# Loading the first queries through ScalarE's queue, without products of ones in gaps, in a newly searched front order

## The chip, the cores and the metric

The kernel runs on one core of a Trainium2 chip. The metric is the device time of one execution in microseconds. A core has TensorE (matrix products; PE in the profile, PEld its weight loads), VectorE (DVE), ScalarE (ACT), GpSimd (POOL) and SyncE (SP, which only issues transfers here). Each engine works through its own list of instructions in order and waits on semaphores of the others. Transfers between the device's memory and the on-chip memory are carried out by 16 DMA engines.

## The reference, cut to what matters

Three layers in a row, in float32, for 2 batches of 768 positions.

```python
# 1: attention, 8 heads of 64: a window of |i-j| < 16, and one summary key and value for each 32 positions
k_sum = k.reshape(B, H, 24, 32, D).max(3);  v_sum = v.reshape(B, H, 24, 32, D).mean(3)
a = softmax([where(window, q @ k.T / 8, -1e9), q @ k_sum.T / 8 + log(32)])
x = a @ [v, v_sum]
# 2: gated layer
u, v = split(relu(x @ w_in));  v = (v - mean(v)) / sqrt(var(v) + 1e-6)
x = (u * (w_spatial @ v + b_spatial)) @ w_out
# 3: gated layer with a 3-tap convolution over positions
h = relu(x @ w_in2);  out = (h * sigmoid(conv3(h))) @ w_out2
```

The weights of layers 2 and 3 come as 64-bit floats; the kernel takes their bits apart itself and holds each as a high and a low float32r part. A product in full precision is three products of such parts.

## The kernel before, in words

**Work of the front.** Attention goes by pairs of heads: pair n (0 to 7; 0 to 3 are batch 0) needs its keys, its queries and its windows of values. `load_kq(n)` loads keys and queries, in two halves each for batch 0 (208 and 192 KB of keys, 192 KB each of queries); `load_values(n)` loads the values' windows in two halves of 288 KB and, for some pairs, the values themselves (384 KB). `keys(n)` scales the windows of keys (L422, L424), takes the maxima of 32 keys (L432) and puts them beside each window (L438). `means(n)` makes the mean values: for pairs 0 and 2 with products on TensorE (L452, for each half of the windows), then L464 and two "puts" (L469, L471), one for each half.

Each pair has two groups; `group(i)` treats six blocks of 64 queries, in these steps:
- scores(i): TensorE, the logarithm and the mask (L496, L503) and q times k (L509), into one of two banks, i mod 2
- row maximum (DVE, L513), six exponentials (ACT, L517), sum and reciprocal (DVE, L520, L523), normalise (L526)
- transposes T(i,0) and T(i,1), three blocks each (PE, L530), into one bank `pt`, each followed by a copy out of it (L552)
- values(i): products with the values (PE, L536), then the high and the low part of the result (L557, L558)

scores(i) needs its bank free, that is the exponentials of group i-2 done; T(i,1) needs the copy of T(i,0) done.

`convert` takes apart one piece of w_in (256 KB for the first four pairs' pieces; L306 load, L307 to L314, L298, L292). Its results feed the products of layer 2 (L344 to L346), which begin while attention still runs and fill TensorE's time between the groups' steps.

**Order.** Every step is entered with `add(engines, rank, reads, writes)` and gets a number. `Plan.order()` emits the steps in the order written in the string `ORDER` (two signs are one number). Each engine's instructions stand in that order. Where a step can run on several engines, `PICK` says on which. The engines' semaphores are set from what is read and written, so that the order decides only who stands behind whom. All loads are steps of "Q", SP's queue.

**Products of ones.** Step 0, `warm(7)`, issues seven products of a tile of ones, 128x512 each, before anything else on TensorE (L1085). Moreover `order()` adds such products in front of a TensorE step where its own cost numbers see TensorE idle for at least 0.5 us, up to the first step of rank 1000 (`plan.fill`):

```python
gap = t - free.get(e, 0.0)
if self.fill and gap >= 0.5:
    n = int((gap - 0.1) / 0.22)
    out.append((free.get(e, 0.0), k, e, 0.22 * n, lambda n=n, f=self.fill[1]: f(n)))
```

In the trace 22 products of ones run: 13 at the start, 5 after scores(0) and 4 after T(1,1).

Of the kernel before, what the change touches and what calls it, by code (L numbers as in the profile page):

```python
# [55 lines left out]
    "AAACABADAFAgAEAiAGAjAZAaAkAhAbAHAqAcAdAeArALBYAfAMBZBbBaBcAIA3A4AsAJAlAtASAUATAVAWAuAvANBiBjAKBEA5A6A7BFCTCRCUBkAmAnAwAx"  # L56
    "AOBvAyAzA8B8CVDJCSBGBwB9DKCbAoApBlBmBnAXDLA9A0A+CcA-BADHDIBxBHBoBRCoBSA1A2BBCdByBzB0BpBqCpBCAYCeAPBdCfCgBDB+DRBrB1B2C1Be"
    "BfBgBhDSEgCqCrCsB3DwEhB-AQCDDeDfB4CEBsChBICWCtBtBuCiDTBKBLEeBJBMBTBNBOCFDgCXCYCjARB5BUCZB6BVCGCHCICJB7C2CAEnETDUDVEoDrCk"
    "CuClCmCnEfCKC3CvCwCaDhDMBPDWBQFNE0DiCxEpCyCzDXC0DYEqErDsCBDxDNDODPBWDjFMDZDaDAC5DtDQFOFPDkDlC6DbDcE1E2DmDnCCDyEUFVDdDoEs"
    "EtDpEuC7C8C9C+C-BXEiDqDBCLFiEvFjE3E4EjEkDzD0EwFvCMCNDuDvCOCPD6DCDDDED7D8D9D1D+D2EEEFD3FBCQEGE5EmDFDGFkEHEIE6D4F6F7EOEPEQ"  # L60
    "ERGmD5F8F9C4FCD-EAEBECFWEXE7FFFGEYEZEaEbGnFHFIFJFKElFXEDE8GlEcEdE9FYFLGkFZFlFaGQGRGDE+ExEJEKELESHPGSGEGFEyFmE-FAFnEzFbFz"
    "F0EMFwGtG6GdEVJwFQFRFcFdF1ENHHHIGeF2F3GfGGGgF4FeHQFSFTF5FoHJFUHRGhGiGjFpFqFrGuFDG7HSHTHKHLEWFsG8GTGUGHF+GVGIFtHMHNFuFfFg"
    "HiHjFxHkHlGJFyG9G+HOHUHXHYGvGKGwHZHVFhHmHWIhGLGMF-GxGyGAHyGBHnIDHzHaGWGXImGCH0FEGoH1HbHcGYHoHqGNGZGaGbHrHsGOGcGPHdG-JtGz"
    "JuIrItIuHtIcG0H2HeGpG1HuIdIiHfIwH3GqG2IsM-INGrJxIOJzGsHvJ3HAIPHBIIHgH4HCInHDG3NBHwG4HEG5IjIvHFIXJ6IJHhJ0IEIYIKNAJ4HGNCIQ"
    "JvIeH5IZJ1IaIbIRIkIFJ5IfIxJyIyIzJBHxJCISJDHpIgILH8I0H+KbJ2H6KBJ8IlITNNKCJEH9H-IMI5H7NDKFI6IBI1I7KDIUIAIoI8JRKcJFKGI9J7NG"
    "NJJGICKHIVKXJ9JHNII2I+I3JSIWJTJUKAKYI-JJJVJIJZJaI4J-JbNEJAJcIpJKKIJWJhKEJLJdJMNFKJNHIqLDJiJeNKLHJXNUJNKQJfIGJjJ+KKJOIHKd"
    "KhJYKRJPJgLIJQKiJmKLLJJoKjNQKSJkKeNLJnLEJpJlJrLFKfKzKlKsKmKtJsKuK0KnKgKZKaLLKMLMK9KTNPLKNMK5LGKkK7LPNOLNK-K+LTNbNRKNLQNS"
    "K6NTNWLXLRLBKvLUNXLOK8LYLZLbKONVNYLVLSNiLcLdNZLALfLgLWNdLeLaKoNeLhLiNaLlLzNcKPNfLCLoL2NpLjKpNgLmNhLpNkL3NlNjLnLkL0L4MOMB"
    "NmJqKqMPMcNnKUMHL1NrNoMQNsNwKrLrNqMINtK1MEMJMRL5MCNuKVMVMdMFNzNvLqNyPXMWKWN3PLMXMDNxK3L6KwL7N0MYN1MeMmPYMnN5K4MfPMMsN2N6"
    "MGK2N4N7LvN+PZPNPaKxN8MoKyN9OAOBMKL9MzMtLsLwN-OCPbMjMuOFPOODPdOHM0PROILxPPMLMkPSOEM7OGOJMpLtPvMqPTMlMrOMPeL+OKPfPQMvOOOL"  # L70
    "OPONOTM3L-MwMxP1P2PpM4OQOUPjMMPkPUPcOaOROWMyLyOVOSMSPlOhPqM5MgM8PVPgP3PWM1MAPmMhOcM9PrOdObM6P7LuP4MZM2MiP8PnQFOXOeM+MaP5"
    "PhPsOkMbQAQGQBPwMNOjL8QCOfOiPiMTMUOoQHQDTXQIP9OYOqOrOpTYOlPtOsQJP+OgPxTdQEP-OmOvPoOtO2PyTeOuPuQXOyP6QYOxQKQcQLQdQMOwOzQZ"
    "O4QaO9O5QeO3PzQbQSQTOnQUQfO6QNQOO-OZQgQVRFO0RAPEQWQPQhPAO7PGO+QuPFP0QQQzO8O1RKQiQjQ0Q1QpTZQvPBQqQRPHQrQsQ2PIQkQwTaQxTjTf"
    "RBRLQlQtRGRcQ3TgQyRCQmQ4TpTrRDRMRHRXRIRNRYQ5TlRZU-RhRiQ6TsQnPCRdThRER2QoTbRJRsRxTiTqRORtRPTcUwRaTkTmT2UxRQQ7RjRyReQ8TtRR"
    "RfTuRzRkR3T3UrPJRTQ9RuPKR4RSR0TnRbQ+RgRlRvR5U1RmSGSLSMT6ToQ-SBRUSfSCR1RwR6PDTvTwR7SDU2SERnSHRVRoRqRpSFU6R8SIR9R+R-UySNSJ"
    "SaSKSbSgRWSORrU7ScVASATCShSQTPTRSdSPTQU8SRSTSkSSTHUzSUSiSVUsSzSlS9SWVBU3U0SmSeS4TSUtSnTJSXVKSYSjSpVLTKSZTxS5TIVDSqSoSrVC"
    "TDS0UuSsS+U9VES1S2TLVMStSuSvVVSxS6S7TTUXVOVGTMTUSwU4URULUdTNS3UlUMVPSyVHU5UYTEUeUSVNUfS-UvT4S8TOUNVWUZVFVgVRUTVXWAVYVrUj"
    "U+TVVcTFVhUUVSV7UVUOVdTAWBT7VIUPV8V3VzV4VQUpVJTGVtViVZVTTWVjVnV0VbWwV1UnWxV5VUTyTzVeVvV6VoV2VmV9VfWCVkT9WDWyW-WEXAV+T-Ua"
    "T5V-UEW1VaWrWMWNW2WFXBUGVlUAWGUmWHUHWzW0WOUkWPWsT0WIVpUgXKVqVsUqWQUhXLWZUoWJT1XDTBWaW6W3WKWTWtXMUbW4XCWuWbXEW7WvXGXHXVXO"
# [1153 lines left out]
```

## Time and profile before

| | |
|---|---|
| three runs | 321.55 us median, 320.36 to 322.11 |
| the profiled execution | 320.81 us; span of its instructions 318.9 us |
| TensorE busy | 311.4 us, 98% of the span |
| VectorE, ScalarE, GpSimd busy | 268.5, 237.3, 117.0 us |
| moved by DMA | 37.64 MB |

The span is the time from the first to the last instruction; 1.9 us of the execution lie around it. A busy share is a mean over the whole span. Each row of the trace starts with its time from the span's start in us and its length in us.

### The profile page before, as it was taken

How to read it: one execution, taken by the hardware profiler on the slowest of the kernel's cores; microseconds unless marked ns; L12 is line 12 of the kernel's file. 1: busy time of each engine (PE TensorE's matmuls, PEld its weight loads, DVE VectorE, ACT ScalarE, POOL GpSimd, SP SyncE). 2: the span in 40 equal slices, each digit the busy share in tenths (PEclk: the TensorE clock that was granted, in tenths of full speed). 3: DMA queues.
4: the chain of work that ended last, by engine and by line, in shares of the span. 5: the costliest groups of instructions: out<-in, count | busy, mean ns of one | idle time of the engine just before them, and what ended most of it. 6: DMA issues, size and time to landing. Idle time of an engine off the chain costs nothing.

```text
span 318.9 us, 6374 instructions
## 1 busy us (share of the span) xinstructions
PE 311.4 (98%) x2376; PEld 271.6 (85%) x2376; DVE 268.5 (84%) x493; ACT 237.3 (74%) x565; POOL 117.0 (37%) x130
## 2 busy tenths in 40 slices
...
GB/s 222 305 266 306 224 218 179 329 93 159 168 189 110 24 2 13 53 29 142 138 114 124 117 134 133 132 2 0 25 21 5 75 25 51 26 99 104 128 140 99
DMA packets 16061, 37.64 MB, mean 118 GB/s; under 512 B 1952, under 2 KB 8480, under 8 KB 16032
## 3 DMA queue, kind: packets, MB, share of 16 engines
...
## 4 chain that ended last, share of the span: by engine, by line
PE 88%; DVE 5%; DMA 2%; SPq 1%; ACT 1%; POOL 1%; issue 1%; DVEq 0%; POOLq 0%
PE late L345 11%; PE late L346 11%; PE late L344 11%; PE mm L344 10%; PE mm L346 9%; PE mm L345 9%; PE pt L530 3%; PE xp L344 3%; PE xp L346 3%; PE xp L345 3%; PE xp L536 3%; PE pt L344 3%; PE pt L346 3%; PE pt L345 3%; PE s L509 2%; DMA a<-q_in 2%
## 5 line engine op out<-in xcount | busy, mean ns | idle before, releaser
L517 ACT ACTIVATE a<-s,a 128x120 f32<-128x120 f32 x96 | 33.3, 379 | 1.0 <-DVE a L513 0.8
L345 PE MATMUL late<-xl,a 128*128 128x512 f32 (+1 forms) x80 | 29.5, 369 | 0.1
L344 PE MATMUL late<-xh,a 128*128 128x512 f32 (+1 forms) x80 | 29.4, 367 | 0.0
L346 PE MATMUL late<-xh,a 128*128 128x512 f32 (+1 forms) x80 | 29.4, 367 | 0.0
L914 DVE SCALAR_TENSOR_TENSOR w<-v,conv_t,w 128x1534 f32<-128x1534 f32 x12 | 21.8, 1817 | 4.4 <-POOL w L908 2.1
...
L526 POOL TENSOR_TENSOR a<-a,a 128x720 f32<-128x720 f32 x14 | 19.4, 1394 | 6.4 <-DVE a L523 3.5
L517 ACT ACTIVATION_READ_ACCUMULATOR a<-s,a 128x1 f32 x96 | 21.6, 225 | 0.0
L292 POOL TENSOR_TENSOR w<-a,w 128x256 fp32r<-128x256 f32 (+2 forms) x13 | 14.2, 1099 | 15.1 <-PE late L345 7.9
L530 PE MATMUL pt<-ident,a 128*120 128x128 f32 x96 | 16.5, 281 | 0.8 <-DVE a L552 0.6
L345 PEld LDWEIGHTS late<-xl,a 128*128 128x128 f32 x80 | 15.0, 188 | 2.4 <-DVE xl L292 0.4
L346 PEld LDWEIGHTS late<-xh,a 128*128 128x128 f32 x80 | 15.0, 188 | 1.9
L344 PEld LDWEIGHTS late<-xh,a 128*128 128x128 f32 x80 | 15.0, 188 | 1.8
L513 DVE TENSOR_REDUCE a<-s 128x6 f32<-128x720 f32 x16 | 14.2, 899 | 2.2 <-PE s L509 2.1
L298 ACT CAST w<-a 128x512 fp32r<-128x512 f32 (+2 forms) x17 | 10.0, 589 | 7.9 <-DVE a L337 3.4
L327 ACT ACTIVATE a<-a 128x512 uint16<-128x512 uint8 x20 | 15.8, 789 | 0.0
L330 ACT ACTIVATE a<-a 128x512 f16<-128x512 f32 x20 | 15.6, 782 | 0.0
L298 ACT CAST xh<-tmp 128x384 fp32r<-128x384 f32 x24 | 12.1, 512 | 3.9 <-DVE tmp L878 2.0
L530 PEld LDWEIGHTS pt<-ident,a 128*120 128x120 f32 x96 | 10.8, 137 | 5.0 <-DVE a L552 1.0
L344 PE MATMUL mm<-w,xh 128*128 128x512 f32 x36 | 14.9, 414 | 0.0
L344 PE MATMUL mm<-xh,a 128*128 128x512 f32 (+1 forms) x40 | 14.7, 367 | 0.0
L346 PE MATMUL mm<-xh,a 128*128 128x512 f32 (+1 forms) x40 | 14.7, 367 | 0.0
...
## 6 DMA issues: line engine op xcount, KB each, us to landing
...
a<-vhalf SPq DMA_DIRECT2D x8, 288.0 KB, 6.9
...
```

What stands on the lines that cost most here:

```text
L292: eng.tensor_tensor(out=lo.r(), in0=src.f(), in1=hi.f(), op=ALU.subtract)
L298: us = {"ACT": (0.2 + n / 1200, lambda: ACT.copy(hi.r(), src.f())), "POOL": (0.12 + n / 1050, lambda: POOL.tensor_copy(hi.r(), src.f()))}
L327: ACT.activation(out=c.ap.bitcast(U16).rearrange("p (n w) -> p n w", w=2)[:, :, 0], in_=byte, func=AF.Copy, scale=1.0 / 32.0, bias=-15.5 / ...
L330: ACT.mul(c.ap.bitcast(F16).rearrange("p (n w) -> p n w", w=2)[:, :, 1], word(), 2.0 ** -60)
L344: PE.matmul(ps, lhsT=lh, rhs=rh, start=first and i == 0, stop=False, **kinds)
L345: PE.matmul(ps, lhsT=lh, rhs=rl, start=False, stop=False, **kinds)
L346: PE.matmul(ps, lhsT=ll, rhs=rh, start=False, stop=last and i == n - 1, **kinds)
L513: DVE.tensor_reduce(out=st[:, 0], in_=sv, op=ALU.max, axis=AX.X, negate=True)
L517: ACT.activation(out=e[:, u, :NK], in_=sv[:, u // GA, u % GA], func=AF.Exp, bias=st[:, 0, u:u + 1], accum_out=sm[:, u, :1])
L526: eng.tensor_tensor(out=e, in0=e, in1=st[:, 1].unsqueeze(2).to_broadcast([128, GB, NK]), op=ALU.mult)
L530: PE.transpose(pt3[:NK, a], e[:, GA * h + a, :NK], ident)
L914: DVE.scalar_tensor_tensor(out=two(ct)[:, bs, to], in0=two(h)[:, bs, of], scalar=scale(k), in1=two(ct)[:, bs, to], op0=ALU.mult, op1=ALU.add)
```

## The change

1. The queries of pair 0 are no longer loaded by SP. Two steps "QA" issue them from ScalarE's instruction list, the first as ScalarE's first instruction.
2. The first use of the exponential, which brings the load of ScalarE's table, becomes a step `table` behind the first of these; the copy of the mask's ones (`one_tile`) waits for it.
3. `plan.fill` goes: no products of ones in gaps. `warm(7)` at the start stays.
4. New strings `ORDER` and `PICK`. With the new step's number counted in, the steps of each engine up to the middle of layer 2's spatial product stand in another order; the last 277 of TensorE's 511 steps stand as before. 78 steps change between VectorE, ScalarE and GpSimd; VectorE gets 461 steps instead of 449, ScalarE 378 instead of 385, GpSimd 116 instead of 120.

SP's loads, before and after, with k for keys, q for queries, v for windows of values, the pair in brackets and the halves as a and b:

```
before: k(0)a k(0)b w_in q(0)a k(1)a k(1)b q(0)b v(0)a w_in q(1)a v(0)b k(2)a k(2)b q(1)b k(3)a q(2)a ...
after:  k(0)a k(0)b k(1)a k(1)b v(0)a w_in w_in q(1)a v(0)b k(2)a k(2)b q(1)b k(3)a q(2)a ...   ScalarE: q(0)a, table, q(0)b
```

TensorE's steps, before and after (means(0)a is the half of the means' products that needs v(0)a):

```
before: warm scores0 scores1 means(0)a scores2 means(0)b T(0,0) scores3 T(0,1) scores4 T(1,0) values0 T(1,1) T(2,0)
        scores5 values1 T(2,1) scores6 T(3,0) mean(1) T(3,1) layer2 scores7 values2 ...
after:  warm scores0 scores1 means(0)a scores2 means(0)b T(0,0) scores3 T(0,1) scores4 T(1,0) values0 T(1,1) scores5
        T(2,0) values1 T(2,1) scores6 T(3,0) mean(1) means(2)a T(3,1) scores7 values2 ...
```

```diff
     def __init__(self):
         self.work, self.seen, self.life = [], {}, {}
-        self.fill = None
...
             if e == "PE":
-                if self.fill and rank >= self.fill[0]:
-                    self.fill = None
-                gap = t - free.get(e, 0.0)
-                if self.fill and gap >= 0.5:
-                    n = int((gap - 0.1) / 0.22)
-                    out.append((free.get(e, 0.0), k, e, 0.22 * n, lambda n=n, f=self.fill[1]: f(n)))
...
         for i in range(qp):
             q0, q1 = S // qp * i, S // qp * (i + 1)
-            dma((q1 - q0) / 2 * 0.84 + (166 if n + i == 0 else 0), lambda q0=q0, q1=q1: SP.dma_start(qts[j].ap[:, q0:q1], q_in[b, p][:, q0:q1]), r - 9 + 1.5 * i, writes=[qts[j].tok(q0, q1)])
+            if n:
+                dma((q1 - q0) / 2 * 0.84, lambda q0=q0, q1=q1: SP.dma_start(qts[j].ap[:, q0:q1], q_in[b, p][:, q0:q1]), r - 9 + 1.5 * i, writes=[qts[j].tok(q0, q1)])
+            else:
+                add({"QA": (1.2 - 0.4 * i, lambda q0=q0, q1=q1: ACT.dma_start(qts[j].ap[:, q0:q1], q_in[b, p][:, q0:q1]))}, r - 100 + i, writes=[qts[j].tok(q0, q1)])
...
     DVE.memset(mhalf, -0.5)
-    ACT.activation(out=stat[0][:, 11:12], in_=mhalf, func=AF.Exp)
...
+    def table():
+        ACT.activation(out=stat[0][:, 11:12], in_=mhalf, func=AF.Exp)
+
...
-    add({"ACT": (2.65, one_tile)}, -99, [tok("ident")], [mask_b.tok(sub="o")])
+    add({"ACT": (2.2, table)}, -99.5, writes=[tok("table")])
+    add({"ACT": (0.6, one_tile)}, -99, [tok("ident"), tok("table")], [mask_b.tok(sub="o")])
...
-    plan.fill = DENSE, warm
```

## Rows read from the trace of the kernel before

**Rows 1.** Part 1 of the page: busy us, share of the span and instructions

```profile
PE 311.4 (98%) x2376; PEld 271.6 (85%) x2376; DVE 268.5 (84%) x493; ACT 237.3 (74%) x565; POOL 117.0 (37%) x130
```

**Rows 2.** Busy us (and instructions) of each engine by stretch, then PEclk, DMA share, GB/s

```profile
2.00:13.05 11.05, 9.61 (x125) 5.11 (x123) 7.40 (x23) 5.99 (x30) 3.96 (x9) 1.00 1.00 279
13.05:17.00 3.95, 3.90 (x78) 3.14 (x82) 3.91 (x9) 3.85 (x18) 3.41 (x5) 1.00 1.02 365
...
40.00:60.00 20.00, 19.89 (x293) 17.29 (x294) 18.50 (x38) 17.82 (x63) 10.10 (x16) 1.00 0.73 232
```

**Rows 3.** The chain that ended last, in order of time: start, us, what

```profile
4.94 7.02 DMA a<-q_in
...
18.68 1.40 POOL a L526
```

**Rows 4.** TensorE in order of time, 0 to 20 us

```profile
1.04 4.55 PE L1085 MATMUL mm<-ones 128*128 128x512 bf16 x13 [1.04 <-DVE mhalf L1079]
...
7.22 1.25 PE L1085 MATMUL mm<-ones 128*128 128x512 bf16 x5
...
13.10 1.49 PE L452 MATMUL mm<-a,a 96*24 96x128 f32 x12 [0.16 <-DMA a<-vhalf]
14.52 0.54 PE L530 MATMUL pt<-ident,a 128*120 128x128 f32 x3
...
18.97 1.03 PE L1085 MATMUL mm<-ones 128*128 128x512 bf16 x4
```

**Rows 5.** TensorE in order of time, 20 to 28 us

```profile
20.60 0.23 PE L496 MATMUL s<-a,ones 64*64 64x72 bf16 x4
...
21.49 0.92 PE L536 MATMUL xp<-a,a 120*64 120x64 f32 x24
...
24.97 0.54 PE L530 MATMUL pt<-ident,a 128*120 128x128 f32 x3 [0.61 <-DVE a L552]
...
26.70 0.92 PE L536 MATMUL xp<-a,a 120*64 120x64 f32 x24
```

**Rows 6.** Transfers issued at 2.10, 4.94 and 5.77 us: KB, us to landing

```profile
a<-q_in SPq DMA_DIRECT2D x1, 192.0 KB, 4.2
...
a<-q_in SPq DMA_DIRECT2D x1, 192.0 KB, 7.0
...
a<-vhalf SPq DMA_DIRECT2D x1, 288.0 KB, 7.3
```

**Rows 7.** SP's issues in order of time: the first two and the eleventh

```profile
0.73 0.86 SPq L397 DMA_DIRECT2D a<-k_in  x2
...
5.77 0.33 SPq L410 DMA_DIRECT2D a<-vhalf  x1
```

**Rows 8.** VectorE and GpSimd in order of time, 14 to 19 us

```profile
14.12 0.97 DVE L432 TENSOR_REDUCE a<-a 128x12 f32<-128x384 f32 x2
15.10 0.56 DVE L552 COPY a<-pt 120x384 f32<-120x384 f32 x1
...
16.04 0.91 DVE L513 TENSOR_REDUCE a<-s 128x6 f32<-128x720 f32 x1
...
16.85 1.74 POOL L471 TENSOR_SCALAR a<-a 24x768 f32<-24x768 f32 x2
```

**Rows 9.** ScalarE in order of time: first and last of the 12 instructions of exponentials(3)

```profile
17.15 0.36 ACT L517 ACTIVATE a<-s,a 128x120 f32<-128x120 f32 x1
...
19.09 0.24 ACT L517 ACTIVATION_READ_ACCUMULATOR a<-s,a 128x1 f32 x1
```

**Rows 10.** Products of ones (L1085) alone, by stretch: us, PE busy, PEld busy, PEclk

```profile
1.04:4.30 3.26, 3.26 (x8) 1.19 (x9) 1.00 0.71 218
7.25:8.40 1.15, 1.15 (x5) 0.37 (x5) 1.00 1.05 258
```

**Rows 11.** TensorE at the end, by stretch: us, PE busy, PEclk

```profile
314.50:318.30 3.80, 0.30 (x2) 1.00 0.33 124
318.45:318.90 0.45, 0.00 (x0) 0.50 0.00 0
```

More of the change, by code (lines that the diff above doesn't have):

```diff
@@ L55 @@
 ORDER = (
[L56 to L79, printed above, removed]
@@ L80 @@
-    "WUWcW8W5WVXNXPXgWWXvXWXXXzXRX3YAWRX4WfT+XFVuX7XSX0T8X5WlUBXYW9YBXhWSXcUcXZUCW+VxXQXiXrWmXdXjX1VwX8WgXnUDX2XIYCX6XoVyUFX9"
-    "WhYDXkYEXtXJX+WnX-XlYMXaYNWXYFUIWLYGUQWdUJXbUKYOXuYHXxXsYIXTWoYPYJXeYTYKXUYQXwYRWiXyWpXmXpWjYZYfYlXfYmUiYgUWWYYLYnYSYoYh"
-    "WeYaYbXqYiYUWkYcYdYpWqYqYVYWYjYXYkYeYY"
+    "ABAIADAJAAAGAHAMACANAKAFAhAEBZAaATAOAjAkALAlArBbAiA4AsBcBaAcAbA5BFBGBdAtAdAPAmA6B9AVAUAuCSBHB+AvAeBjAWAnBIBkBSCVAQAwB-Ax"
+    "CUBwA7AoCTBlA8AyBxCWA9BmApAzA0CcA+ByDKA1BnDLA-BTBABoBBCdA2CeAqDIBzCpC2BpDMA3BCB0BqBDCAARB1CqCEBeCfDJBrEgBsDSCrBEB2BfCgBJ"
@@ new lines @@
+    "CXB3BgBLEhBKChAXCsB4BiBhDfASEfBtC3DTAYCYCtBMCBBNAZBuB5CuBvEiDUDgBOEUDVCZCiCjBPBUCGCaB6CkEoClCFB7B8DhCHCvCmDsEpCwCICbDiCL"
+    "DWCxBQE1DXCnCoCyEqDjCJCzC0C4CCBRDYDNDBFPDtDZFNC1DaDODkDxCKErDyDbC6DlDPEsFQC8CDDQDmDzFODRDcDnDoE2DdEtDuE3EuC7DeBVDpAfC9C+"
+    "EvBWEVC-DqFWFjDADrE4EwEjFwBXFCD0GlD1E5ExAgDvFkEkC5CMDwD7E6FDD8FlGnCNBYCODCCPD9CQDDD+D2FXDEE7D3D4D-CRDFD5F9EYElEFE8D6F8E9"
+    "FYEGEZDGEHEADHFGEBEaGoEbF+FHFZEnEcF0EIECFIF7EdEDE+FmGRFJEeF1EmGEGSE-EyEEEJFAFaEPFKFbF2EQGFFxFnEzFLGmFBERGTF3ESGeE0GUEWEK"
@@ new lines @@
+    "ELFoEMETGGFcFRENFdFMGVF4G7GuFSGfFeEOGgHQFfHRF5FTGhGiF6JxFpHIGHFqHJG8GjFEFrFVF-HKHSGkGIEXG9FyHLFsFUHTFtHMFgHUGvG+HYFzGWFh"
+    "FuFvFiGwGJGKGLHjGAHkGMHZHNInGNGXIoHVGYGBIdHWGDGxIeGZHOHXFFGaG-GyHaJuHlHmGbGCGcIsGzHnHPGOIuGpHbGdHcGPIvG0GQIpG1HzG2GqIxHA"
+    "G3IfHdH0HeHBHCHrGrH1HoItHfH2H3GsHDHsIJIKGtILNAH4HEHtNCHuHgHFHGG4IiHHITJ4HvHwIwHpHqNBIUJ1IVNDHhH5IMJyIqIWIgHxJ2IhIjH6KCG5"
+    "HyIkG6IlNOKDKEH7ImHiKGKHIYINH-H9KcKIIOIZKFH+JzIaIXIbIcKYIPIEIyNEJ7J0KZIQNHJ3H8IzIFNJI0IRIAI6IBISKdI1I2JCJ6I7JSJTJ5JUJ9I3"
@@ new lines @@
+    "IGICI8I9JDJENFJFI4J8NKI+J+IDNGJKJGJaI-JVI5JbJHJWJLNIJMNLJcJAJIJJJBJiJdIrJeJXJNJjKKKJJOKLLEKRKSJfKeJYKTJkJPJZJgIHLFJhJQNM"
+    "JRK0JlKfKMLIJnIIK1JpJmKaKiNRNQJoKmKtKbNNKgJqLJLGNPJsNSJtKjKkKnKoNTLKKlLHKhKuLQLRK6K+K7K-KvLMK8LNK9LOLSLPLTLLKANUNVLUNWNX"
+    "NcNYLVLcNjLALYLdKBNZLWJ-LeKNJvNaLBKULgKOLhLZLXLaKPNeLCLfLbKpNfLiLjNbLmL0KwNdKQNgLDLpL3NqLkKqNhLnNiLqNlL4NmNkLoLlL1L5MPMC"
+    "NnJrKrMQMdNoKVMIL2NsNpMRNtNxKsLsNrMJNuK2MFMKMSL6MDNvKWMWMeMGN0NwLrNzPYMXKXN4PMMYMENyK4L7KxL8N1MZN2MfMnPZMoN6K5MgPNMtN3N7"
@@ new lines @@
+    "MHK3N5N8LwN-PaPOPbKyN9MpKzN+OBOCMLL+M0MuLtLxOAODPcMkMvOGPPOEPeOIM1PSOJLyPQMMMlPTOFM8OHOKMqLuPwMrPUMmMsONPfL-OLPgPRMwOPOM"
+    "OQOOOUM4MAMxMyP2P3PqM5OROVPkMNPlPVPdObOSOXMzLzOWOTMTPmOiPrM6MhM9PWPhP4PXM2MBPnMiOdM+PsOeOcM7P8LvP5MaM3MjP9PoQGOYOfM-MbP6"
+    "PiPtOlMcQBQHQCPxMOOkL9QDOgOjPjMUMVOpQIQETYQJP+OZJwOrOsOqTZOmPuOtQKP-OhPyTeQFQAOnOwPpOuO3PzTfOvPvQYOzP7QZOyQLQdQMQeQNOxO0"
+    "QaO5QbO+O6QfO4P0QcQTQUOoQVQgO7QOQPPAOaQhQWRGO1RBPFQXQQQiPBO8PHO-QvPGP1QRQ0O9O2RLQjQkQ1Q2QqTaQwPCQrQSPIQsQtQ3PJQlQxTbQyTk"
@@ new lines @@
+    "TgRCRMQmQuRHRdQ4ThQzRDQnQ5TqTsRERNRIRYRJRORZQ6TmRaVARiRjQ7TtQoPDReTiRFR3QpTcRKRtRyTjTrRPRuRQTdUxRbTlTnT3UyRRQ8RkRzRfQ9Tu"
+    "RSRgTvR0RlR4T4UsPKRUQ+RvPLR5RTR1ToRcQ-RhRmRwR6U2RnSHSMSNT7TpRASCRVSgSDR2RxR7PETwTxR8SEU3SFRoSIRWRpRrRqSGU7R9SJR+R-SAUzSO"
+    "SKSbSLScShRXSPRsU8SdVBSBTDSiSRTQTSSeSQTRU9SSSUSlSTTIU0SVSjSWUtS0SmS+SXVCU4U1SnSfS5TTUuSoTKSYVLSZSkSqVMTLSaTyS6TJVESrSpSs"
+    "VDTES1UvStS-U+VFS2S3TMVNSuSvSwVWSyS7S8TUUYVPVHTNTVSxU5USUMUeTOS4UmUNVQSzVIU6UZTFUfUTVOUgTAUwT5S9TPUOVXUaVGVhVSUUVYWBVZVs"
@@ new lines @@
+    "UkU-TWVdTGViUVVTV8UWUPVeTBWCT8VJUQV9V4V0V5VRUqVKTHVuVjVaVUTXVkVoV1VcWxV2UoWyV6VVTzT0VfVwV7VpV3VnV+VgWDVlT+WEWzXAWFXBV-UA"
+    "UbT6WAUFW2VbWsWNWOW3WGXCUHVmUBWHUnWIUIW0W1WPUlWQWtT1WJVqUhXLVrVtUrWRUiXMWaUpWKT2XETCWbW7W4WLWUWuXNUcW5XDWvWcXFW8WwXHXIXW"
+    "XPWVWdW9W6WWXOXQXhWXXwXXXYX0XSX4YBWSX5WgT-XGVvX8XTX1T9X6WmUCXZW+YCXiWTXdUdXaUDW-VyXRXjXsWnXeXkX2VxX9WhXoUEX3XJYDX7XpVzUG"
+    "X+WiYEXlYFXuXKX-WoYAXmYNXbYOWYYGUJWMYHURWeUKXcULYPXvYIXyXtYJXUWpYQYKXfYUYLXVYRXxYSWjXzWqXnXqWkYaYgYmXgYnUjYhUXWZYMYoYTYp"
```

5 lines of the change are left out of this document (3 added, 2 removed).

## The prediction

> **What bounds the kernel now.** I read the busy shares first: TensorE works 98% of the span [rows 1], so a gain must come from the little time in which it has nothing to do, or does work that nobody needs. The stretches place that time: between 2.00 and 13.05 us TensorE counts 9.61 us as busy, part of it products of ones, and between 40 and 60 us it is busy 19.89 us of 20, which leaves 0.11 us to take [rows 2]. From there on nothing but its own products orders its time, and their number does not change. So only the front counts, and I read the chain of waits there: SP issues transfers, the tenth of them, q(1)a, takes 7.02 us from 4.94 to 11.96, then scores(2), VectorE, GpSimd's normalise(2) from 18.68 to 20.08 [rows 3], and right behind it T(2,0) on TensorE. The chain does not run over q(0)a, the transfer that the change moves; scores(0) waits for it, but what follows is overtaken by the later landings.
>
> **What TensorE could lose in the front.** Of the products of ones, 5 run at 7.22 for 1.25 us and 4 at 18.97, until normalise(2) lets T(2,0) start at 20.1 [rows 3, 4]; a later stall of 0.61 us stands before T(3,1) at 24.97 [rows 5]. Behind 14.52 that makes about 1.15 + 0.61 = 1.8 us that a better order can take without earlier data. What lies before 14.52 can be taken only if data come earlier: means(0)b starts at 13.10, held by the landing of v(0)b, 5.77 + 7.3 = 13.07 [rows 4, 6, 7], and T(0,0) follows at 14.52.
>
> **The change part by part.**
>
> *q(0) by ScalarE's queue.* Before, q(0)a lands at 2.10 + 4.2 = 6.3 [rows 6]. By ScalarE it can be issued at about 0.73, as SP's first transfer is [rows 7], and share with k(0). The two k(0) halves are 400 KB, with q(0)a 592. At the rate of 279 GB/s [rows 2] the 196,608 bytes of q(0)a delay k(0)b by 0.7 us at most, q(0)b by as much again if it is issued at once. scores(0) then starts some 0.5 us earlier than before. But what bounds the rest is the sum: in both orders exactly the same eleven transfers, 400 + 384 + 400 + 512 + 192 + 576 = 2464 KB, must land before means(0)b can end, and 2176 KB before scores(2). The DMA engines' share between 2.00 and 13.05 is 1.00 [rows 2], so they never rest. If bytes are what counts, q(1)a lands at 11.96 and v(0)b at 13.07 again, and the gain of this part is 0. If instead ScalarE's queue finds room beside SP's, SP has 393,216 bytes less to carry, and both land 393,216 / 279,000 = 1.41 us earlier. A point for room: the rate is 365 GB/s from 13.05 to 17.00 at the same share [rows 2], so a share of 1 is not the highest rate. Bounds: 0 to 1.41 us. I take 0.3, near the lower end, because the share is the row nearest to the case. The Trainium skill ("DMA: Bandwidth & Descriptors", section "Issuing engines are not separate DMA queues") speaks against this edit: transfers issued by several engines run on the same 16 DMA engines and interleave, and only the issuing time is saved. By that rule the landing term is 0 and the sum below 0.3 instead of 0.6.
>
> *ScalarE's own time.* Two issues of 0.43 us each, as SP's pair takes 0.86 [rows 7], go ahead of its copy of the mask's ones and the first windows of keys. These need k(0)b, which lands after 4 us, so it costs nothing; without that cover up to 0.86 us would stand before scores(1).
>
> *w_in behind the first values.* VectorE has a w_in step ahead of the row maximum of group 1. w_in's first piece is now the eighth transfer by bytes and not the third; VectorE, in order, waits with it, and the row maxima and sums behind it wait too. I find row maximum(1) at about 10.2 to 11.1, as late as before, so the earlier scores(0) and scores(1) win nothing there. Price: nothing, as long as scores(2) waits for q(1)a; if that came 1.41 us earlier this would be late next.
>
> *No products of ones.* 6 of the first 13 go; the engine then waits for k(0) and q(0) anyway: 0. The 5 at 7.22 stand before transfers that land later: 0. The 4 at 18.97 fill a wait and are not its cause: 0. What they may keep up, the clock, is a rival below.
>
> *The order behind 13 us, step by step.* VectorE: row maximum(2) ends at 13.9 as before; two maxima of keys 0.97 [rows 8], sum, mean values and reciprocal(1), which I take at 0.6 together, copy 0.56, row maximum(3) 0.91 [rows 8]: ends at 17.0 (before 16.95). ScalarE: exponentials(3) then run from about 17.15 to 19.33 [rows 9], as before. GpSimd: one put (half of 1.74 [rows 8]) moves behind normalise(2), which can end at 17.8 + 1.40 = 19.2 instead of 20.08 [rows 3]. TensorE: scores(5) is now ahead of T(2,0) and fills the hole: it needs its bank, free at 19.33, takes 21.49 - 20.60 = 0.9 [rows 5] and ends at 20.2; T(2,0) ends at 20.7. Before, both were done at 21.49: 0.8 us ahead. Then VectorE, which has the copy of T(2,0) behind row maximum(4) and the parts of values(0), gives some back: T(2,1) about 21.7, scores(6), which needs exponentials(4), about 22.4, T(3,0) 23.3. The mean of pair 1 needs the bank that VectorE reads last for values(1): about 24.3, half a microsecond of stall again. With one half of means(2), 1.4, T(3,1) 0.5 and scores(7) 0.9, values(2) starts at 27.4. Before it starts at 26.70 [rows 5], with 0.54 of layer 2 more and the 1.4 of means(2) less done: at equal work 26.70 - 0.54 + 1.42 = 27.6. The order gains 0.2 to 0.5; I take 0.3. Ends: all 1.8 us of stalls gone, or, if VectorE's 12 steps more (18.50 us of 20 busy from 40 to 60 [rows 2]) open new ones, about -0.8, the part of its idle time there that half a microsecond per ten would use up.
>
> *Tail.* Same order for the last 277 steps; it starts earlier by the front's gain and nothing else.
>
> **Sum.** 0.3 + 0.3 = 0.6 us, against the profiled execution's 320.81: 320.2. The median of the three runs is 0.74 higher, 321.55, so 320.9 for a median. Half a percent, 1.6 us, is about what a measurement here can tell from no change.
>
> **The rivals.**
>
> *A, the forecast:* the same bytes hold the same landings; gain -0.3 to 1.4 us. For it: share 1.00 and the chain through a transfer that waits in the queue [rows 2, 3]. Chance 0.56.
>
> *B, ScalarE's queue finds room:* q(1)a and v(0)b come 1.41 us earlier and TensorE's closed stretch starts at 13.1 instead of 14.5. With the order's 0.3 that is 1.7, with all stalls gone 1.4 + 1.8 = 3.2: 319.8 down to 318.4 for a median. For it: 365 GB/s at the same share [rows 2]; against it: the share itself. Chance 0.26.
>
> *C, slower: TensorE's clock comes up late.* The first eight products of ones take 3.26 us, 0.41 each, and the five from 7.25 on 0.23 [rows 10]: the first run at the 1.2 GHz level, the later at 2.4, though the clock column reads 1.00 in both; it does not record the low level of the start. At the end the granted clock is 0.50, the 1.2 GHz level, at 318.45, with no product after 314.8 [rows 11]. The change leaves seven products, 7 x 0.41 = 2.9 us from 1.04 to 3.9, then a wait to almost 6, and holes of about two microseconds before v(0)a. If the low level still holds when q(1)a lands at 11.96, scores(2) 0.9 and means(0)b 1.42 take twice as long and T(0,0) is 2.3 us late; if it ends between them, 1.1. Minus 0.6 that gives 322.1 to 323.3. It decides from the point where scores(2) itself runs at the low level. The Trainium skill ("TensorE: Matmul & The Clock Gate", "Part 1: The HAM clock gate") says that the slow clock is the default, that activity lifts it and idleness brings it back; the trace shows both ends of that. Against C: scores(0), scores(1) and means(0)a still come in between and pauses of two microseconds are shorter than those 3.6 at the end. Chance 0.10.
>
> *D, the order costs cover:* landings as in A, but VectorE's added steps stall TensorE between 20 and 100 us: -0.2 to -2, some 322.0. Chance 0.08.
>
> **Chances and range.** Faster by over 0.5%: an eighth of A, 0.07, and nearly all of B, 0.23: 0.30. Slower: six tenths of C and half of D, 0.10. The same: 0.60. The range leaves out the far ends of B and C: 318.7 to 322.4.
>
> **What would show it.** Right: q(1)a lands within 0.4 us of 11.96 and v(0)b of 13.07, T(0,0) starts between 14.0 and 14.6, scores(5) before T(2,0) near 19.3, values(2) near 27. Row maximum(1) waits for w_in. B: T(0,0) near 13.1 and the DMA rate between 2 and 12 us above 320 GB/s. C: means(0)b longer than its 1.49 [rows 4]. D: idle times of TensorE behind 28 us, released by VectorE. Wrong also if the landings of k(0)b go beyond 5.5 us, which would put scores(0) later than before.

## The result, and the profile after

The changed kernel takes 323.57 us (median of 8 runs, 322.51 to 324.87) beside 320.74 us of the kernel before (8 runs, 320.00 to 322.11). The ratio is 1.0085, 95% interval 1.0061 to 1.0109: slower by 0.85%, 2.8 us. The prediction, 320.9 us with a range from 318.7 to 322.4 and a chance of 0.1 for slower, is wrong. The profiled execution took 323.84 us, its span is 322.0 us.

The page's first part of the kernel after, busy us and share of the span, answers to [rows 1]:

```profile
PE 311.4 (97%) x2361; PEld 270.4 (84%) x2361; DVE 281.7 (87%) x505; ACT 231.9 (72%) x557; POOL 120.1 (37%) x126
```

TensorE counts 311.4 us as before, although 15 products of ones are gone. VectorE has 12 instructions more and is busy 13.2 us longer. Twelve instructions of half a microsecond would be 6: so others have become longer.

The stretches of the kernel after, in the columns of [rows 2]:

```profile
2.00:13.05 11.05, 9.59 (x127) 6.59 (x126) 8.28 (x22) 6.37 (x30) 5.11 (x10) 1.00 1.04 348
13.05:17.00 3.95, 2.67 (x71) 1.94 (x70) 3.89 (x12) 3.07 (x17) 2.33 (x4) 1.00 0.93 328
40.00:60.00 20.00, 19.50 (x301) 16.60 (x301) 19.29 (x40) 17.85 (x61) 8.49 (x13) 1.00 0.67 218
```

Between 2 and 13.05 us the transfers move 348 GB/s, where it was 279 [rows 2]. TensorE now loses time in the two later stretches: 1.3 us of 3.95, and 0.5 of 20, where VectorE is busy 19.29 us of 20.

The issues of q(0) and q(1)a, and us from issue to landing of the latter and of v(0)b (to set beside [rows 6, 7]):

```profile
0.72 0.41 ACTq L396 DMA_DIRECT2D a<-q_in  x1
...
1.22 0.39 ACTq L396 DMA_DIRECT2D a<-q_in  x1
...
4.34 0.44 SPq L394 DMA_DIRECT2D a<-q_in  x1
```

```profile
a<-q_in SPq DMA_DIRECT2D x1, 192.0 KB, 5.5
...
a<-vhalf SPq DMA_DIRECT2D x1, 288.0 KB, 5.6
```

q(1)a lands at 4.34 + 5.5 = 9.8 (11.96 before), v(0)b, issued at 5.10, at 10.7 (13.07 before). So the landings are 2.1 and 2.4 us earlier, more than rival B's 1.41.

TensorE in order of time, 0 to 16 us, answers to [rows 4]:

```profile
1.04 3.17 PE L1080 MATMUL mm<-ones 128*128 128x512 bf16 x7 [1.04 <-DVE mhalf L1075]
...
5.89 1.48 PE L505 MATMUL s<-a,a 64*64 64x120 f32 x24 [1.23 <-DVE a L434]
...
11.49 1.49 PE L448 MATMUL mm<-a,a 96*24 96x128 f32 x12
12.91 0.54 PE L526 MATMUL pt<-ident,a 128*120 128x128 f32 x3
...
15.63 0.54 PE L526 MATMUL pt<-ident,a 128*120 128x128 f32 x3 [1.28 <-DVE a L548]
```

T(0,0) starts at 12.91, 1.6 us earlier than before (14.52 [rows 4]). Then T(0,1) waits 1.28 us for VectorE's copy of T(0,0), L548. Why that copy is late is seen in the rows of VectorE, and of GpSimd at the same time:

```profile
9.76 0.41 DVE L305 SCALAR_TENSOR_TENSOR a<-a,a 128x256 uint32<-128x256 uint32 x1
...
10.77 0.19 DVE L519 RECIPROCAL a<-a 128x6 f32<-128x6 f32 x1
10.88 0.38 DVE L307 SCALAR_TENSOR_TENSOR a<-a,a 128x256 uint32<-128x256 uint32 x1
11.18 1.61 DVE L305 SCALAR_TENSOR_TENSOR a<-a,a 128x256 uint32<-128x256 uint32 x1
12.71 0.90 DVE L509 TENSOR_REDUCE a<-s 128x6 f32<-128x720 f32 x1
...
15.06 0.52 DVE L548 COPY a<-pt 120x384 f32<-120x384 f32 x1
...
26.72 1.60 DVE L285 TENSOR_TENSOR w<-a,w 128x256 fp32r<-128x256 f32 x1
...
39.45 1.65 DVE L420 TENSOR_SCALAR a<-a 128x576 f32<-128x576 f32 x1
```

```profile
11.11 1.40 POOL L522 TENSOR_TENSOR a<-a,a 128x720 f32<-128x720 f32 x1 [1.40 <-DVE a L519]
12.48 0.84 POOL L420 TENSOR_SCALAR a<-a 128x576 f32<-128x576 f32 x1
...
26.62 1.42 POOL L522 TENSOR_TENSOR a<-a,a 128x720 f32<-128x720 f32 x1
...
39.23 1.56 POOL L522 TENSOR_TENSOR a<-a,a 128x720 f32<-128x720 f32 x1 [0.54 <-DVE a L519]
```

Each of the three long VectorE instructions starts while GpSimd's normalise (L522) runs, and ends 0.28 to 0.31 us after it: 12.79 after 12.51, 28.32 after 28.04, 41.10 after 40.79. The w_in instruction L305 takes 0.41 us at 9.76, where GpSimd runs nothing beside it, and 1.61 at 11.18. The row maximum of 12.71, which reads the scores from PSUM, runs beside GpSimd's windows and keeps its 0.90. The Trainium skill ("SBUF — State Buffer", section "Who interferes with whom") has the rule: a VectorE instruction with two inputs in SBUF cannot run beside a GpSimd instruction that reads SBUF; whichever starts first keeps the shared ports for its whole length, and the other is blocked. The rows agree for L305 and L285, whose two inputs are in SBUF, and for the untouched row maximum. L420, a tensor_scalar, has one input and is blocked too; the same section names tensor_scalar among the operations that can take the shared ports with a single input, in a faster mode, and no row here shows whether L420 ran in it.

In the kernel before, the same two engines at the same place, VectorE first:

```profile
11.37 0.43 DVE L312 SCALAR_TENSOR_TENSOR a<-a,a 128x256 uint32<-128x256 uint32 x1
11.83 0.43 DVE L314 SCALAR_TENSOR_TENSOR a<-a,a 128x256 uint32<-128x256 uint32 x1
12.17 0.18 DVE L523 RECIPROCAL a<-a 128x6 f32<-128x6 f32 x1
```

```profile
12.51 1.39 POOL L526 TENSOR_TENSOR a<-a,a 128x720 f32<-128x720 f32 x1 [2.81 <-DVE a L523]
```

There the w_in pieces stand ahead of the reciprocal that releases the normalise, so they cannot meet it. The new order puts L307 and L305 behind the reciprocal. The planner keeps steps marked lock=True on the two engines apart in its own reckoning of time (free["LOCK"]), but nothing in the program does: normalise(0) needs the reciprocal alone and starts as soon as that is done.

Summed over the VectorE instructions that took over 0.15 us more than the usual time of their line and shape, the excess is 0, 1.4 and 3.0 us (to 20, 20 to 100, 100 to 160 us) before, and 1.2, 7.0 and 7.6 us after.

How far TensorE is ahead of the kernel before, in us, worked out in each profile as the time gone less the products done, each product at its usual time at the full clock, and then the difference from the kernel before (what is taken for the usual times moves a value by up to 0.3 us, at 14 us by up to 0.8):

| at us | 14 | 17 | 35 | 95 | 155 | 250 |
|---|---|---|---|---|---|---|
| after | +1.8 | +0.2 | 0.0 | -1.0 | -2.3 | -2.3 |
| e1 | +0.5 | +0.3 | +0.6 | +0.6 | +0.4 | +0.5 |
| e15 | +2.3 | +2.1 | +1.5 | +0.3 | -0.9 | -0.9 |
| e16 | +2.1 | +1.8 | +2.5 | +1.8 | +0.7 | +0.7 |
| e13 | +1.9 | +1.4 | +2.0 | +1.6 | -3.3 | -3.4 |
| e8 | -0.2 | -0.2 | 0.0 | +0.2 | -3.1 | -3.2 |

So the front won what rival B said, and the first meeting took it by 17 us. What the table leaves out is that the order then won again: values(2) starts at 26.34 us, and the prediction reckons 27.6 for the kernel before at equal work, so TensorE stood 1.2 us ahead. That was lost by 35 us behind the second meeting, the w_in part of 26.72; here it stands in the chain that ended last (start, us, what), ahead of the transposes that wait for the copy:

```profile
26.80 1.52 DVE w L285
28.32 0.48 DVE xh L553
...
31.91 0.48 DVE a L548
32.43 0.54 PE pt L526 x3
```

Between 35 and 155 us another 2.3 us went. Behind 250 us the profiled execution lost 1.0 us more, which goes with one late transfer (last section).

### The profile page after: what moved, and what is told of

Same layout as the page of the kernel before. It is cut to its first block, busy times and chain, and to the rows that moved or that the text cites. A ratio compares the mean times of both kernels' runs of the same rounds, so it can differ in the third digit from the quotient of the medians.

```text
span 322.0 us, 6365 instructions
## 1 busy us (share of the span) xinstructions
PE 311.4 (97%) x2361; PEld 270.4 (84%) x2361; DVE 281.7 (87%) x505; ACT 231.9 (72%) x557; POOL 120.1 (37%) x126
## 4 chain that ended last, share of the span: by engine, by line
PE 72%; DVE 16%; DMA 3%; ACT 3%; issue 3%; POOL 2%; SPq 0%; DVEq 0%; POOLq 0%
PE late L337 9%; PE late L338 9%; PE late L339 9%; PE mm L337 8%; PE mm L338 8%; PE mm L339 8%; PE xp L338 3%; PE xp L337 3%; PE xp L339 3%; PE pt L526 2%; PE s L505 2%; PE pt L338 2%; PE pt L337 2%; PE pt L339 2%; PE xp L532 2%
## 5 line engine op out<-in xcount | busy, mean ns | idle before, releaser
L522 POOL TENSOR_TENSOR a<-a,a 128x720 f32<-128x720 f32 x14 | 20.3, 1454 | 6.2 <-DVE a L519 6.0
L285 DVE TENSOR_TENSOR a<-a,a 128x256 fp32r<-128x256 f32 (+2 forms) x20 | 18.7, 943 | 0.0
L326 POOL TENSOR_SCALAR a<-a 128x512 f32<-128x512 f32 x7 | 10.8, 1549 | 14.1 <-DMA a<-w_out 9.0
L291 ACT CAST xh<-tmp 128x384 fp32r<-128x384 f32 x24 | 12.1, 512 | 5.2 <-DVE tmp L874 3.3
L603 POOL TENSOR_TENSOR stat<-stat,mhalf 128x1 f32<-128x1 f32 x12 | 9.8, 844 | 14.4 <-DVE stat L600 14.4
L505 PE MATMUL s<-a,a 64*64 64x120 f32 x384 | 14.0, 281 | 1.2 <-DVE a L434 1.2
```

Of the source, the lines that this page charges most:

```text
L285: eng.tensor_tensor(out=lo.r(), in0=src.f(), in1=hi.f(), op=ALU.subtract)
L505: PE.matmul(sv[c * QB:(c + 1) * QB, h, a], lhsT=qts[j].ap[rows, blk * QB:(blk + 1) * QB], rhs=kws[j].ap[rows, blk * NK:(blk + 1) * NK], st ...
L522: eng.tensor_tensor(out=e, in0=e, in1=st[:, 1].unsqueeze(2).to_broadcast([128, GB, NK]), op=ALU.mult)
```

## The experiments

Theory S: VectorE and GpSimd meet where the new order lets them, and the blocked VectorE makes TensorE wait. Rivals: the clock (C), the earlier landings alone (L), and the order itself, whether the engines meet or not (O). In the edits, `new` and `old` are the two orders as lists of step numbers (`old` with the table load as step 3); a step keeps the engine of the list that it is taken from.

**e1, the old order with q(0) moved.**

```diff
-seq = new
+seq = [8, 3, 9] + [k for k in old if k not in (8, 3, 9)]
```

> The order and the engines of the kernel before, with the one change that q(0)a and q(0)b go through ScalarE's queue (its table load between them), and without products of ones. Theory S (the new order puts VectorE's and GpSimd's steps on top of each other; earlier landings do no harm): 319.3 to 320.7 us, as fast as before or up to 1.4 us faster, with VectorE's steps between 20 and 100 us not longer than in the kernel before. Rival L (earlier landings alone upset the work behind them): 322 us or more, TensorE's stalls behind 30 us as in the changed kernel.

320.53 us beside 320.73, ratio 1.0019 (0.9990 to 1.0048): no difference. The stretch from 2 to 13.05 us:

```profile
2.00:13.05 11.05, 9.94 (x126) 6.79 (x124) 8.34 (x23) 6.50 (x32) 4.14 (x9) 1.00 1.04 332
```

332 GB/s: moving q(0) alone raises the rate. L falls, and the profile's lead of 0.5 us stays to the end; in the median it cannot be told from nothing. q(1)a landed at 10.12 us and v(0)b at 11.29, yet T(0,0) starts at 13.90: in the old order most of the earlier landings is not used.

**e2, the products of ones again.**

```diff
+    plan.fill = DENSE, warm
```

> The changed kernel with the products of ones put back into the planned gaps of TensorE. Rival C (the clock comes up late without them): TensorE's full clock again from about 4.4 us and 321.5 us or less. Theory S: nothing is gained, 323.2 to 324.0 us, whatever the clock does before 9 us, since scores(0) and scores(1) wait for landings in both.

323.13 us, ratio 1.0069 (1.0046 to 1.0091). scores(0) takes 0.79 us at its full rate, and the time is still that of the changed kernel: C is not the cause of the loss.

**e3, the new front and the old rest.**

```diff
-seq = new
+seq = new[:145] + [k for k in old if k not in new[:145]]
```

> The first 145 steps in the order of the changed kernel (to about 28 us), everything behind them in the order and on the engines of the kernel before. Theory S with the damage behind the front: TensorE keeps its lead of about 1.4 us at 26 us, 319.3 to 320.7 us. If the damage sits in the front itself, or if any shift of the front upsets the rest: 322 us or more.

321.75 us, 1.0035 (1.0007 to 1.0063), between the two cases. The lead that the front brings is gone by 35 us here too, in the stalls of T that wait for the copy. (The profiled execution, 320.88 us, is the fastest of its twelve.)

**e4, GpSimd behind VectorE to the 985th step.** GpSimd's locked steps wait for the last locked VectorE step written ahead of them.

```diff
-        for *_, fn in done:
-            fn()
+        ahead = None
+        for n, (_, k, e, _, fn) in enumerate(done):
+            ins = fn()
+            if plan.work[k][3] and e == "POOL" and ins and ahead and n < KEEP:
+                tc.add_manual_dep(ins.ins, ahead.ins.name, mybir.DependencyInfo(mybir.DependencyClass.Sync, mybir.DependencyReason.SCHED_ONLY), reason="planned order")
+            if plan.work[k][3] and e == "DVE" and ins:
+                ahead = ins
```

> The changed kernel, in which each of GpSimd's steps that the planner keeps apart from VectorE's (to the 985th step) also waits for the last of VectorE's such steps ahead of it in the written order. Theory S: VectorE's instructions that took 1.6 us in place of 0.4 (11.2, 26.7, 39.5, 62.6 us and others; 8.2 us of excess before 100 us) are back at their own length, and the time falls to 321 to 322.3 us, about half of the loss or more; GpSimd's waits give some of it back. Rival O (the order is worse whether the two engines meet or not, since VectorE has more steps early): 323.2 us or more.

327.92 us, 1.0236: slower still. VectorE's excess to 100 us fell from 8.2 to 1.4 us, and TensorE was level with the kernel before at 95 us; but the waits cost two stalls of 1.1 and 1.9 us between 99 and 104 us, and more behind. A wait holds up GpSimd's whole queue, so where it stands matters.

**e5, the waits to 44 us; e6, with the old rest behind; e7, the new order to 97 us and the old rest; e8, the reverse.**

```diff
-KEEP = 985
+KEEP = 250
```

> The changed kernel, with GpSimd's steps waiting for VectorE's as in e4, but only to the 250th step of the written order (about 44 us). Theory S: the long VectorE instructions at 11.2, 26.7, 30.6 and 39.5 us are gone, TensorE stands 1.0 to 1.3 us further at 45 us than in the changed kernel, and the time is 322.0 to 322.6 us. Rival O (the order is worse whether the two engines meet or not): 323.1 us or more.

```diff
-seq = new
+seq = new[:250] + [k for k in old if k not in new[:250]]
```

> The first 250 steps in the order of the changed kernel with those waits, the rest in the order and on the engines of the kernel before. Theory S: the lead of about 1.1 us at 45 us stays to the end: 319.3 to 320.2 us, faster than both kernels. Rival K (something behind 45 us, a transfer or VectorE's own work, takes up any lead): 320.4 to 321.3 us.

```diff
-seq = new
+seq = new[:525] + [k for k in old if k not in new[:525]]
```

> The first 525 steps (to about 97 us) as in the changed kernel without any added wait, the rest as in the kernel before. If half of the loss lies behind 97 us, where 19 steps went to another engine: 321.8 to 322.5 us. If it all comes from ahead of 97 us: 323.1 us or more.

```diff
-seq = new
+seq = old[:525] + [k for k in new if k not in old[:525]]
```

> The first 525 steps in the order of the kernel before (with q(0) through ScalarE's queue), the rest in the order and on the engines of the changed kernel: the counterpart of e7. If the part behind 97 us costs by itself: 321.4 to 322.2 us. If it costs only because the front has shifted it: 320.3 to 320.9 us.

e5: 322.47 us, 1.0059 (1.0032 to 1.0087), about 1 us less than the changed kernel, as S said, though the two intervals overlap. e6: 320.60 beside 320.75, 0.9996 (0.9976 to 1.0017), the kernel before's time, as its rival K said: in its profile the rest of the old order keeps 0.7 us of lead to 250 us, and a late transfer near 298 us takes it (last section). e7: 324.41, 1.0129, in its second case and above the changed kernel; e8: 323.37, 1.0095, outside both of its cases. Either half of the new order, joined to the other half of the old, costs about as much as the whole or more, so the losses of the halves do not add up. e8 shows that the new rest loses 3.3 us from 95 to 155 us behind a front that is as before.

**e9, the 18 steps behind 97 us on their old engines; e10, with the waits of e5; e11, e7 with them; e12, the changed kernel again.**

```diff
-engine[k] = new_engine[k]
+engine[k] = old_engine[k] if k in new[525:] else new_engine[k]
```

> The changed kernel in its own order, but the 18 steps behind 97 us that went to another engine are back on the engines of the kernel before. If those choices make VectorE and GpSimd meet there (7.6 us of stretched VectorE time between 100 and 160 us, 3.0 before): 322.2 to 322.8 us. If it is the order and the phase, not the engines: 323.1 us or more.

> The waits of e5 (GpSimd behind VectorE, to 44 us) and the engines of e9 together. If the two causes add up: about 1.1 us less than e9, 321.0 to 321.8 us. If not: as e9 or e5, 322.2 us or more.

> As e7 (new order to 97 us, the rest as before), with the waits of e5 to 44 us. Theory S with an early front: the rest, no longer late, runs as in the kernel before and the lead of 1 us is kept: 319.4 to 320.4 us. Rival P (the rest fits only the phase it was written for, and any join there costs): 322.5 us or more.

> The changed kernel once more, as the measure for e9 to e11 on the same chip: 323.0 to 323.9 us. If the VectorE instructions stretched are those of the profile at hand only, another execution would show others; theory S expects the same ones (11.2, 26.7, 39.5 us) again.

e12: 323.26 us, 1.0077 (1.0054 to 1.0099), with the same long instructions (1.61 us at 10.94 and 26.49, 1.65 at 39.39): they belong to the program, not to one execution. e9: 331.84 us, 1.0361, a miss by 9 us: VectorE's excess between 100 and 160 us did fall, 7.6 to 4.1, but TensorE waits elsewhere, first for VectorE 2.04 us:

```profile
102.92 0.80 PE L338 MATMUL late<-xl,w 128*128 128x512 f32 x1 [2.04 <-DVE xl L554]
```

(There are 18 such steps; e7's expectation says 19.) The engines belong to the order; this edit says nothing for or against S behind 97 us. e10: 330.07, 1.8 us below e9, so the early waits help by as much there. e11: 323.04, 1.0070: the join costs again, as its rival P said.

**e13, the waits to 90 us and from 120 to 153 us; e14, only the later; e15, one wait.**

```diff
-n < KEEP
+any(i <= n < j for i, j in KEEP)
```

KEEP is ((0,480),(600,725)) in e13, ((600,725),) in e14, ((57,58),) in e15.

> The changed kernel with GpSimd's steps waiting for VectorE's in two stretches of the written order: steps 0 to 479 (to about 90 us) and 600 to 724 (about 120 to 153 us), without the stretch in which e4 paid 3.3 us at 100 to 104 us. Theory S: below e5 by what the meetings at 80 to 84 and 141 to 150 us cost in the changed kernel (0.5 and 0.5 to 1.0 us): 320.8 to 322.0 us. Rival O (behind 44 us the order itself is the cost): 322.3 us or more.

> The changed kernel with those waits in steps 600 to 724 alone. Theory S: TensorE's loss of 1.0 us between 140 and 155 us is gone, 322.2 to 322.8 us. Rival O: 323.1 us or more, with the loss in the same place.

> The changed kernel with one added wait: normalise(0) on GpSimd behind the VectorE instruction of w_in (L305) that took 1.61 us at 11.18. Theory S: that instruction takes 0.43 us, T(0,0) starts about 0.25 us later, but the stall of 1.5 us ahead of T(0,1) shrinks to 0.5 us or less, and TensorE stands about 1 us further at 17 us. In the end 322.4 to 323.2 us, as later stalls take part of it. Rival: the stall stays at 1.5 us, since the copy ahead of T(0,1) waits for something else.

e15: 322.10 us, 1.0052 (1.0027 to 1.0077), where the changed kernel has 1.0085 and 1.0077: by the ratios one wait on one instruction is worth 0.8 to 1.1 us, by the medians 1.3 to 1.7 (1.1 us above its before, where the changed kernel is 2.4 to 2.8 above). Each of these ratios is known to within 0.8 us, so the times say some 1 us and no more. VectorE, GpSimd and TensorE of e15:

```profile
9.80 0.19 DVE L519 RECIPROCAL a<-a 128x6 f32<-128x6 f32 x1
9.90 0.39 DVE L307 SCALAR_TENSOR_TENSOR a<-a,a 128x256 uint32<-128x256 uint32 x1
10.20 0.42 DVE L305 SCALAR_TENSOR_TENSOR a<-a,a 128x256 uint32<-128x256 uint32 x1
10.64 0.91 DVE L509 TENSOR_REDUCE a<-s 128x6 f32<-128x720 f32 x1
...
13.00 0.52 DVE L548 COPY a<-pt 120x384 f32<-120x384 f32 x1
```

```profile
10.77 1.39 POOL L522 TENSOR_TENSOR a<-a,a 128x720 f32<-128x720 f32 x1 [1.65 <-DVE a L305]
```

```profile
12.21 0.55 PE L526 MATMUL pt<-ident,a 128*120 128x128 f32 x3 [0.21 <-POOL a L522]
...
13.59 0.54 PE L526 MATMUL pt<-ident,a 128*120 128x128 f32 x3
```

The instruction of 1.61 us takes 0.42, the row maximum follows at once, the copy no longer waits behind it, and T(0,1) starts without a stall. This does not hang on the one execution, nor on the rate at which scores(0) ran: T(0,1) follows T(0,0) by 2.4 to 2.7 us in the profiles of the changed kernel's front without this wait (after, e7, e9, e12, e14) and by 1.4 us in those with it (e4, e5, e10, e11, e13, e15, e16, e17), and both groups have executions with scores(0) in 0.84 and in 1.48 us.

e13: 325.99 and e14: 327.15, both misses, for one reason. Up to 145 us e13 is 1.6 us ahead of the kernel before; then one of the later waits holds GpSimd for 14.9 us, and TensorE stands still for 3.4 us behind it (the granted clock, 1.00 from 140 to 148 us, is 0.50, the 1.2 GHz level, from 151.6 to 153):

```profile
143.73 1.28 POOL L285 TENSOR_TENSOR v<-a,v 128x512 fp32r<-128x512 f32 x1 [14.91 <-DVE a L712]
```

```profile
151.67 0.66 PE L337 MATMUL late<-a,a 128*128 128x384 f32 x1 [3.37 <-ACT xh L291]
```

**e16, the waits to 90 us alone; e17, and one more at 142 us; e18, e17 with 11 products of ones.**

KEEP is ((0,480),) in e16, ((0,480),(728,729)) in e17 and e18, and in e18:

```diff
-WARM = 7
+WARM = 11
```

> The changed kernel with GpSimd's steps waiting for VectorE's to the 479th step (about 90 us) and nowhere behind. Theory S, as e13 stood to 145 us (TensorE 2.8 us further than in the changed kernel and 1.5 us further than in the kernel before): behind 145 us it loses the 1.0 to 1.2 us that the changed kernel loses there, and ends at 319.9 to 321.0 us, at or a little below the kernel before. Rival O (the order itself costs, and what is won ahead of 90 us is taken up behind): 322.0 us or more.

> As e16, and the GpSimd sum (L712) that the VectorE instruction of 2.2 us met at 142 us waits as well. Theory S: 0.3 to 0.8 us below e16, 319.3 to 320.5 us. If that wait holds up GpSimd's later steps, as the waits of e13 did at 151.7 us: 1 us or more above e16.

> As e17, with 11 products of ones at the start in place of 7 (they end near 5 us, before scores(0) can start). In 8 of 17 profiles of kernels with 7 products scores(0) ran at the low clock (12 products in 1.48 us for 0.84), and with the added waits T(0,0) then came 1.2 us later (e4, e10, e17 against e5, e13, e15, e16). If the clock is what is left of the loss: scores(0) in 0.84 us in every execution, T(0,0) near 12.6 and 319.8 to 320.8 us, 0.6 us or more below e17. If not: 321.2 to 321.8 us, as e16 and e17.

e16: 321.65 us, 1.0041 (1.0018 to 1.0063), half of the loss is gone, 0.6 us less of it than expected. e17: 321.44, 1.0019 (0.9999 to 1.0039), 0.9 us above what was expected; e18: 320.88, 1.0013 (0.9990 to 1.0035), the time of the kernel before within the measurement. The steps from e16 to e17 and to e18 are smaller than the intervals, so what the one more wait and the four more products are worth is not shown. The profiled execution of e18, 324.26 us, had a lower mean granted clock (0.989) and is not compared with the others; it shows what C described: after a wait of 2.24 us for v(0)a scores(2) takes 1.48 us and means(0)b 2.75, and T(0,0) starts at 16.34.

e17 and e16, scores(0) and T(0,0) on TensorE:

```profile
6.42 1.48 PE L505 MATMUL s<-a,a 64*64 64x120 f32 x24 [1.76 <-DVE a L434]
...
13.72 0.54 PE L526 MATMUL pt<-ident,a 128*120 128x128 f32 x3 [0.21 <-POOL a L522]
```

```profile
5.59 0.84 PE L505 MATMUL s<-a,a 64*64 64x120 f32 x24 [1.28 <-DVE a L434]
...
12.33 0.54 PE L526 MATMUL pt<-ident,a 128*120 128x128 f32 x3
```

With seven products of ones, scores(0) took 1.48 us, the length of the 1.2 GHz level, in 8 of 17 profiled executions and 0.84 or 0.85 in the others, after the same seven products; the clock column reads 1.00 in both.

To 100 us e16 and e17 are the same program, and yet the product that TensorE begins at 95.02 us in the changed kernel begins at 92.08 in e16 and at 93.80 in e17, whose k(0)b landed 0.8 us later and whose scores(0) was slow. So the 2.8 us between after and e16 in the table are too much for the waits. With scores(0) in 1.48 us this product begins at 94.97 to 95.22 without the waits (after, e12, e14) and at 93.80 and 94.01 with them (e17, e4); with scores(0) in 0.85 or 0.84 us at 94.31 and 94.52 (e9, e7) and at 92.36 and 92.08 (e13, e16). The waits gain 1.0 to 1.4 us here in the first group and 1.9 to 2.4 in the second.

Where the gain lies is the same in every profile, counted from one product of TensorE to another in the same order. At the second meeting, the changed kernel and e16:

```profile
28.61 0.54 PE L526 MATMUL pt<-ident,a 128*120 128x128 f32 x3
...
33.83 0.50 PE L337 MATMUL mm<-xh,w 128*128 128x512 f32 x1
```

```profile
27.18 0.54 PE L526 MATMUL pt<-ident,a 128*120 128x128 f32 x3
...
31.19 0.50 PE L337 MATMUL mm<-xh,w 128*128 128x512 f32 x1
```

That is 5.2 us and 4.0; it is 5.0 to 5.4 in the six profiles without the waits there (after, e7, e9, e12, e14, e15) and 4.0 in the seven with them (e4, e5, e10, e11, e13, e16, e17). From 79.05 to 95.02 us, where e5, e10 and e11 have no waits either, it is 15.9 to 16.0 us without and 15.3 or 15.4 with.

## Why the prediction was wrong, point by point

**What bounds the kernel**: right that only the front could be won, wrong that nothing behind it orders TensorE's time but its own products. VectorE at 18.50 us of 20 [rows 2] was one blocked instruction from ordering it. The base of the forecast was also 0.8 us high: 321.55 us for three runs, 320.74 for eight.

**The landing term**, 0.3 of 0 to 1.41 us: mis-sized. It measured 1.6 us at T(0,0), with the landings 2.1 and 2.4 us earlier; over the seven profiles of this front without added waits T(0,0) is 1.4 to 2.4 us early. The move of q(0) alone brings the rate from 279 to 332 GB/s (e1), but it takes the new order to use it: in the old one T(0,0) starts at 13.90 (e1) and 14.71 us (e8), with q(1)a and v(0)b 1.8 to 2.3 us earlier in both. The share of 1.00 [rows 2] was no sign of a full line, as 365 GB/s at the same share in the next stretch had said. By the rule of the Trainium skill that the prediction cites ("DMA: Bandwidth & Descriptors", section "Issuing engines are not separate DMA queues") only the issuing time is saved. The trace does not agree: q(1)a is issued 0.6 us earlier, and from issue to landing it takes 5.5 us where it took 7.02.

**ScalarE's own time, the products of ones**: right as terms of nothing; with the products of ones the time is 323.13 us (e2). C's mechanism occurred, scores(0) took 1.48 us at the low level, but T(0,0) was early all the same; so C did not make the loss. It has a price, though: at the product of 95.02 us the profiles with the slow scores(0) stand 0.5 to 0.9 us behind the others without the waits, and 1.4 to 1.9 with them; there k(0)b also landed later (5.2 and 5.5 us in e4 and e17, 4.6 in e13 and e16), and the two are not told apart.

**The tail**, "the front's gain and nothing else": not so in the profiles. The same last products take 19.5 us before, 20.5 in the changed kernel and 19.8 in its second profile (e12), with the landing of one transfer (last section). How much of the 2.8 us of the medians this is, is not shown, since the kernel before has one profile.

**w_in behind the first values**: the row maximum of group 1 did not wait for w_in; it starts at 8.94 us, 1.1 earlier than before (10.07). What the step left out is where the pieces of w_in went instead: behind the reciprocal, where one of them met normalise(0).

**The order**, +0.3 of -0.8 to +1.8: the step that failed. TensorE's own sequence is as forecast, scores(5) ahead of T(2,0) at 18.97 us (19.3 said) and values(2) at 26.34 (27 said). That the second came so near is luck: the landings had given 1.6 us where 0.3 was said, and the first meeting had taken most of it. The step summed VectorE's steps each at its own length, and put only the added ones on the scales. It did not ask which GpSimd instruction runs at that moment. What the order cost in the profile by 155 us is 4.1 us: from 1.8 ahead to 2.3 behind. Of this, what goes before 95 us is the meetings. Product by product they cost 1.0 to 1.3 us between T(0,0) and T(0,1), 1.0 to 1.4 between 28.61 and 33.83 us and 0.6 between 79.05 and 95.02; the waits that take them away give some of it back elsewhere, and leave the same order 1.0 to 2.4 us further at 95 us (e4, e17, e13, e16). The first meeting alone, at 11.2 us, is worth some 1 us of the time (e15).

**Rival D** named VectorE and the place, "between 20 and 100 us", with 0.08 and some 322.0; the mechanism it lacked is the block, and its stretch begins at 11 us. A and D left out that two theories can hold at once: B's landings came true, and D's cost was larger.

**Open.** Behind 97 us the changed kernel loses 1.3 us against the kernel before. There are long VectorE instructions there too (5.16 us for two at 110.05), but e13 and e14 could not take the meetings away without a worse wait, and e9 changed the engines and with them everything else; that these meetings are the cause there, and not the order itself (O), is argued, not shown. Only one of them has a price: with the one more wait of e17, at 142 us, TensorE goes from the product at 140.08 us of the changed kernel to the one at 155.03 in 14.6 us, where it takes 14.9 to 15.0 without (after, e5, e12, e15, e16). The clock's share in the last 0.5 us is not shown either.

No version beats the kernel before by more than the measurement tells: the nearest are e6 (0.9996), e18 (1.0013), e1 and e17 (1.0019 both).
